# Three of the last four output sets by adding DMAs: x written ahead from SyncE's queue, the gated part added from GpSimd's

## The chip, the cores and the metric

The kernel runs on one core of a Trainium2 chip. The core has TensorE (PE, matrix multiply), VectorE (DVE), ScalarE (ACT), GpSimd (POOL) and SyncE (SP), which here only issues DMAs. DMAs are issued from the instruction queues of SP, ACT and POOL and are carried out by 16 DMA engines that all three share. The metric is the device time of one execution in microseconds; lower is better.

## The reference

With x of 2048 tokens by 576 channels, all in fp32:

```python
xn = _layernorm(x)
s = _A_ref(xn, ...)          # a long convolution along the tokens: y + u * D_skip
g = _silu(_B_ref(xn, ...))   # layernorm, Dense 576 -> 4608, gelu, Dense 4608 -> 576, + b2
return x + s * g
```

So each output element is x plus a gated part, s times silu(z), where z is the output of the multi-layer perceptron (MLP).

## The kernel before, in words

The 2048 tokens are held as 16 sets of 128. The MLP runs over them in two halves (sets 0 to 7, then 8 to 15), each in 12 groups of 384 hidden channels, and each group in two blocks of four sets: 48 slots. A slot has three first-layer units (L595, into PSUM tiles `mxa` and `mxb`) and eight second-layer units (L658); their results are added to `acc` (L668). fp32 operands are split into a high and a low fp32r part, so each product is three matmuls.

The convolution runs beside it in six chunks of 96 channels, through PSUM tiles `cv`, and its matmuls are laid between those of the MLP. Each chunk has steps on TensorE named `x1`, `k1`, `s2` (four times, L1136, each with its own constants `f2t`, loaded at L1024), the inverse (twice, L1178, with constants `g2t`, loaded at L1027) and `i1`. `f2t` has one buffer: a load waits until TensorE is done with the old constants, and TensorE waits for the load. The result of a chunk goes to `s_s` in memory.

The order of all instructions is written out when the program is built: a planner (`Order`) with an estimated time for each step decides what is put next into which engine's queue, and every queue is pinned to that order. Each engine then carries out its own queue in that order and waits there on semaphores. `last_x(k)` counts in the planner as a step of no engine that takes 9 us, for any k.

For the last eight sets, 8 + k with k = 0 to 7, `last_x(k)` loads x into `TM[k]` (L715, on SP's queue), and `last_s(k)` loads s (L720) once the last chunk is done. In the last two slots `finish` ends each set as soon as its `acc` is complete: `act_z` on ScalarE (L738), for sets 8 to 11 a tanh with two products on VectorE (L745, L749), for sets 12 to 15 a silu with one product on VectorE (L743); then `total`, an addition of x on VectorE (L753) and two stores of 64 rows each into the output (L756), both on SP's queue, or for sets 14 and 15 one on SP's and one on ACT's. Set 15 is done in two halves of 288 channels, taken straight from PSUM. Sets 0 to 7 are combined earlier and stored from POOL's queue (L709). The raw weights are loaded on SP's queue (L513, L515, L518), and so is a small copy of `XR` (L569).

Of the kernel before, what the change touches and what calls it, by code (L numbers as in the profile page):

```python
# [9 lines left out]
F32 = mybir.dt.float32  # L10
# [3 lines left out]
OP = mybir.AluOpType  # L14
# [3 lines left out]
L, D, N, F = 2048, 576, 128, 4608  # L18
P = 128
# [12 lines left out]
NXC, NROW = 1, 4  # L32
# [3 lines left out]
TB = 512  # L36
# [3 lines left out]
def dve(n):  # L40
    return 0.075 + 0.00104 * n


def act(n):
    return 0.06 + 0.00098 * n
# [160 lines left out]
def step(eng, dur, fn, need=(), mark=None, cv=0, at=0.0, late=0.0, tbl=None, by=1e9):  # L206
    return dict(eng=eng, dur=dur, fn=fn, need=tuple(need), mark=mark, cv=cv, at=at, late=late, tbl=tbl, by=by)
# [3 lines left out]
def mixer_kernel(ctx, tc, u, log_a_real, a_imag, c_real, c_imag, log_dt, d_skip, w1, b1, w2, b2,  # L211
                 f1, f2, g2, g1, tvals, ident, out, parts=("mlp", "s4d")):
    nc = tc.nc
    sb = ctx.enter_context(tc.tile_pool(name="sb", bufs=1))
# [8 lines left out]
    def dram(ap_of, offset, ap):  # L223
        return bass.AP(tensor=ap_of.tensor, offset=ap_of.offset + offset, ap=ap)
# [135 lines left out]
    def table_memory():  # L360

        t = [sb.tile([P, 2, SB, NV], F32, name="w", bufs=2) for _ in range(2)]
        t = [x.rearrange("p k c t -> p (k c t)") for x in t + [sb.tile([P, 2, SB, 64], F32, name="v")]]
        return [t[k // 3][:, k % 3 * D:(k % 3 + 1) * D] for k in range(8)]
# [326 lines left out]
    def rows_at(t, b, c0, c1):  # L691
        return [dram(t, (b + 16 * y) * D + c0, [[32 * D, 64], [1, c1 - c0]]) for y in range(2)]
# [18 lines left out]
    def last_x(k):  # L711

        if k == 0:
            TM.extend(table_memory())
        nc.sync.dma_start(TM[k], u_s[:, 8 + k, :])  # L715

    def last_s(k):

        m = A2F[:, k * D:(k + 1) * D]
        nc.sync.dma_start(m, s_s[:, 8 + k, :])  # L720
        XS[8 + k] = (TM[k], m)

    TM = []

    def load_identity():
        IDM[0] = sb.tile([P, 32, 24], F32, name="xc", bufs=NXC).rearrange("p b d -> p (b d)")[:, :P]
        nc.sync.dma_start(IDM[0], ident)

    def finish(b, c0, c1, silu, end, z=None):

        c = slice(c0, c1)
        z = acc[:, b - 8, c] if z is None else z
        n = c1 - c0
        T = []

        def act_z():
            T.append(sb.tile([P, D], F32, name="row", bufs=NROW)[:, c])
            nc.scalar.activation(T[0], z, AF.Silu if silu else AF.Tanh, scale=1.0 if silu else 0.5)  # L738

        def mul():  # L740
            s = XS[b][1][:, c]
            if silu:
                nc.vector.scalar_tensor_tensor(s, s, 2.0, T[0], op0=OP.mult, op1=OP.mult)  # L743
            else:
                nc.vector.tensor_mul(s, s, z)  # L745

        def mul2():
            s = XS[b][1][:, c]
            nc.vector.scalar_tensor_tensor(s, T[0], 1.0, s, op0=OP.add, op1=OP.mult)  # L749

        def total():
            x, s = XS[b]
            nc.vector.tensor_add(x[:, c], x[:, c], s[:, c])  # L753
            for y, o in enumerate(rows_at(out, b, c.start, c.stop)):
                queue = nc.scalar if end and y else nc.sync
                queue.dma_start(o, x[64 * y:64 * y + 64, c])  # L756
        st = [step("ACT", act(n), act_z, tbl="silu" if silu else "gelu"), step("DVE", dve(n), mul)]
        if not silu:
            st.append(step("DVE", dve(n), mul2))
        return st + [step("DVE", dve(n), total)]  # L760


    def params():
# [705 lines left out]
    for k in range(8):  # L1469
        tl["steps"].append(step(None, 9.0, lambda k=k: last_x(k), need=[("kg", NB - 1), ("u", NT - 1)], mark=("x8", k)))  # L1470
# [102 lines left out]
    for slot in range(NSLOT):  # L1573
# [3 lines left out]
        n = slot // 2  # L1577
        final = slot >= NSLOT - 2
        for pos in range(NPOS):
            if pos < G:  # L1580
# [9 lines left out]
                if pos == 2:  # L1590
                    BEGUN.clear()
                    k = slot % (2 * NG)
# [14 lines left out]
            else:  # L1607
# [12 lines left out]
                b = 8 + 4 * tb + j  # L1620
                if halves:
                    dh = terms[0][1]
                    od.marks["z", dh] = od.t["PE"] + od.LAT
                    x = od.line()
                    x["steps"] += finish(b, dh * 288, dh * 288 + 288, True, True, cell[0])
                    x["steps"][0]["need"] = (("z", dh), ("s8", b - 8))
                elif last:
                    add = cell[0]
                    chain = [step("DVE", dve(D), lambda: add(0, 2), mark=("acc", slot, j), by=add_by(pos, j))]
                    if final:  # L1630
                        x = el if slot < NSLOT - 1 else od.line()
                        st = finish(b, 0, D, slot == NSLOT - 1, slot == NSLOT - 1 and j > 1)
                        st[0]["need"] = (("acc", slot, j), ("s8", b - 8))
                        x["steps"] += st
                    elif g == NG - 1:
                        for d in range(2):
                            one, two = gate_store(4 * tb + j, d)
                            by = od.t["PE"] + 5.0
                            chain += [step("ACT", act(288), one, tbl="gelu", by=by), step("DVE", dve(288), two, by=by)]
                    od.urgent.append((od.t["PE"], chain))  # L1640
# [61 lines left out]
```

## Time and profile before

| | us |
|---|---|
| median of 3 runs (1101.43 to 1102.87) | 1101.46 |
| the profiled execution, its own time | 1101.22 |
| span of its trace, first to last instruction | 1099.4 |
| TensorE busy in it | 1090.6 |
| VectorE busy | 919.5 |
| ScalarE busy | 696.6 |
| GpSimd busy | 184.2 |

The profiled execution took 1101.22 us, 1.8 us more than its span; it lies 0.24 us under the median. Times in the trace count from the start of the span. TensorE is busy for 99% of it, at a mean granted clock of 0.998 of full speed. Matmuls overlap and their ends are modelled, so the sum of durations is larger than what a stretch takes.

### The profile page before, as it was taken

Reading aid. Unit: us, or ns where it says so; the run is one execution under the profiler, and the core shown is the slowest. Engines: PE = TensorE matmul, PEld = TensorE weight load, DVE = VectorE, ACT = ScalarE, POOL = GpSimd, SP = SyncE. Lnnn points to the kernel's source line nnn. Section 1 sums busy time; section 2 is a strip of 40 time slices with the busy share of each in tenths; the row PEclk is TensorE's granted clock in tenths of the full one; section 3 lists DMA queues with packets and bytes.
Section 4 is the critical chain, followed back from the end, with each engine's and each line's share of the span. In section 5 each row is a group of like instructions: output and inputs, shape, how many; then the busy total and the mean of one; then the engine's idle time right before and its main releaser. Section 6 shows DMA issues by size and latency. Waiting matters only on the chain.

```text
span 1099.4 us, 27205 instructions
## 1 busy us (share of the span) xinstructions
PE 1090.6 (99%) x11447; PEld 954.3 (87%) x11447; DVE 919.5 (84%) x1514; ACT 696.6 (63%) x1040; POOL 184.2 (17%) x254
## 2 busy tenths in 40 slices
PE   9999999999999999999999999999999999999997
PEld 7989899889888888888998888888888888888896
DVE  7798668979998899999999998898998986766356
ACT  6585699866666675676765857566675754324233
POOL 5566211160110100001100000000100012110320
PEclk9999999999999999999999999999999999999999
DMA  8746745734434141355623314241333426453453
GB/s 236 229 150 149 252 141 197 216 73 128 154 119 150 48 112 57 109 120 151 150 56 91 95 56 126 39 146 61 90 92 77 144 65 180 117 177 111 125 148 94
DMA packets 139683, 138.23 MB, mean 126 GB/s; under 512 B 88952, under 2 KB 105016, under 8 KB 138984
## 3 DMA queue, kind: packets, MB, share of 16 engines
q1 hardware_dynamic: 124664, 85.49, 28.9%
q0 software_dynamic: 14336, 50.12, 14.6%
q8 instruction: 89, 1.46, 0.5%
q10 hardware_dynamic: 560, 0.89, 0.3%
q14 instruction: 34, 0.28, 0.1%
HBM read 102.17 MB, written 36.63 MB: 126 GB/s over the span
## 4 chain that ended last, share of the span: by engine, by line
PE 97%; DVE 2%; ACT 1%; issue 0%; DMA 0%; ACTq 0%; DVEq 0%
PE mxb L658 21%; PE mxa L658 21%; PE mxa L595 20%; PE mxb L595 20%; PE cv L1136 3%; PE cv L971 3%; PE cv L1178 2%; PE cv L1204 2%; PE cv L1106 1%; PE cv L1075 1%; PE mxa L610 0%; PE cv L478 0%; DMA acc<-in_A_u_dram 0%; DVE st L403 0%; PE mxa L578 0%
## 5 line engine op out<-in xcount | busy, mean ns | idle before, releaser
L637 DVE TENSOR_TENSOR hl<-h,hh 128x512 fp32r<-128x512 f32 x144 | 98.7, 690 | 90.7 <-ACT hh L634 90.1
L658 PE MATMUL mxb<-w2h,hh 128*128 128x288 f32 x576 | 171.8, 298 | 0.0
L658 PE MATMUL mxa<-w2h,hh 128*128 128x288 f32 x573 | 170.9, 298 | 0.0
L658 PE MATMUL mxb<-w2h,hl 128*128 128x288 f32 x576 | 170.2, 295 | 0.0
L658 PE MATMUL mxb<-w2l,hh 128*128 128x288 f32 x576 | 169.7, 295 | 0.0
L658 PE MATMUL mxa<-w2h,hl 128*128 128x288 f32 x573 | 169.3, 296 | 0.0
L658 PE MATMUL mxa<-w2l,hh 128*128 128x288 f32 x573 | 168.8, 295 | 0.0
L631 ACT ACTIVATE h<-mxa,b1t 128x512 f32<-128x512 f32 x73 | 50.0, 687 | 111.6 <-PE mxa L595 110.8
L658 PEld LDWEIGHTS mxa<-w2h,hh 128*128 128x128 f32 x573 | 107.7, 188 | 6.6 <-issue 3.5
L658 PEld LDWEIGHTS mxb<-w2h,hh 128*128 128x128 f32 x576 | 108.2, 188 | 5.7 <-issue 1.8
L658 PEld LDWEIGHTS mxb<-w2l,hh 128*128 128x128 f32 x576 | 108.2, 188 | 0.6
L658 PEld LDWEIGHTS mxa<-w2l,hh 128*128 128x128 f32 x573 | 107.7, 188 | 0.7
L658 PEld LDWEIGHTS mxb<-w2h,hl 128*128 128x128 f32 x576 | 108.2, 188 | 0.0
L658 PEld LDWEIGHTS mxa<-w2h,hl 128*128 128x128 f32 x573 | 107.6, 188 | 0.0
L872 POOL DMA_DIRECT2D par<-par_s x36 | 27.8, 771 | 463.7 <-DVE mg L915 458.9
L634 ACT ACTIVATE hh<-h 128x512 fp32r<-128x512 f32 x144 | 90.5, 631 | 3.6
L631 ACT ACTIVATE h<-mxb,b1t 128x512 f32<-128x512 f32 x71 | 48.8, 688 | 68.4 <-PE mxb L595 67.7
L668 DVE TENSOR_TENSOR acc<-mxa,acc 128x576 f32<-128x576 f32 x87 | 65.5, 752 | 31.3 <-PE mxa L658 31.1
L595 PE MATMUL mxa<-XH,w1h 128*128 128x512 f32 x284 | 79.1, 400 | 0.0
L595 PE MATMUL mxb<-XH,w1h 128*128 128x512 f32 x280 | 78.0, 400 | 0.8 <-DVE acc L668 0.7
L668 DVE TENSOR_TENSOR acc<-mxb,acc 128x576 f32<-128x576 f32 x88 | 66.1, 751 | 14.7 <-PE mxb L658 14.4
L595 PE MATMUL mxa<-XL,w1h 128*128 128x512 f32 x284 | 76.1, 390 | 0.0
(260 smaller groups left out, 2486.7 us busy)
## 6 DMA issues: line engine op xcount, KB each, us to landing
raw<-in_B_w_dram SPq DMA_DIRECT2D x72, 288.0 KB, 3.4
raw<-in_B_w_dram SPq DMA_DIRECT2D x96, 192.0 KB, 3.5
par_s<-A POOLq DMA_DIRECT2D x4, 2160.0 KB, 8.1
par<-par_s POOLq DMA_DIRECT2D x36, 240.0 KB, 3.4
f2t<-f2q SPq DMA_DIRECT2D x24, 256.0 KB, 3.3
g2t<-g2p SPq DMA_DIRECT2D x24, 256.0 KB, 3.9
bias<-XR SPq DMA_DIRECT2D x42, 128.0 KB, 3.6
raw<-in_B_w_dram SPq DMA_DIRECT2D x48, 96.0 KB, 3.6
```

Of the source, the lines that this page charges most:

```text
L595: nc.tensor.matmul(q, a, b, start=j == 0 and i not in BEGUN, stop=j == len(ops) - 1, skip_group_check=True)
L631: nc.scalar.activation(t, q, AF.Gelu_apprx_tanh, bias=b1t[:, k:k + 1], scale=1.0)
L634: LAST[0] = nc.scalar.activation(hh[:, i], t, AF.Copy)
L637: nc.vector.tensor_sub(hl[:, i], t, hh[:, i].bitcast(F32))
L658: nc.tensor.matmul(q[:, dh, :288], a[:, i, c], b[:, i, d], start=i == 0 and k == 0 and not alone, stop=i == G - 1 and k == 2)
L668: nc.vector.tensor_add(o, q[:, dh:dh + n, :288], b)
L872: nc.gpsimd.dma_start(PAR[b].rearrange("p (g i) k -> p g (i k)", g=4), dram(par_s, (b // 3 * 48 + b % 3 * 4) * NPAR, [[D * NPAR, P], [12 * ...
L971: nc.tensor.matmul(q[32 * g:32 * g + 32, i // 2, i % 2 * 64:i % 2 * 64 + 64], U[:, ri, 4 * g + i, :], v[:, ri, 4 * g + i, :], start=ri == ...
L1075: nc.tensor.matmul(Q[24 * v][:, e], FP[0][r, f, 0], x[r, 12 * e:12 * e + 12], start=n == 0, stop=n == 2, skip_group_check=True)
L1136: nc.tensor.matmul(Q[i][32 * q:32 * q + 32, f, 2 * ri:2 * ri + 2], m[r, 4 * i + q, 32 * ri:32 * ri + 32], A2[r, 4 * p + 2 * i + q // 2, :, ...
L1178: nc.tensor.matmul(QI[q // 2][64 * f:64 * f + 64, q % 2, i], MAT["g2t", p + i // 2][r, i % 2, f, ri], YS[p + i // 2][0][r, i % 2, ri, f], ...
L1204: nc.tensor.matmul(Q[h][64 * y:64 * y + 64, t], g1t.rearrange("p a e -> p (a e)"), A2[:, k:k + 2, 1].rearrange("p i d r -> p i r d"), star ...
```

## The change

For k = 4, 5 and 6 (sets 12, 13 and 14) `last_x` issues, right behind the load of x into `TM[k]`, two stores from `TM[k]` into the rows of the output, on the same queue (SP). At the end `total` no longer adds x on VectorE for these sets and no longer stores from SP or ACT: it issues two DMAs of 64 rows each from GpSimd's queue that add the gated part to the output in memory. In the planner this `total` counts as 1.6 us of GpSimd instead of an addition on VectorE. Beside that, the silu of the two halves of set 15 goes into a buffer of the ring `h32` (2 buffers) instead of the ring `row` (4 buffers).

```diff
@@ last_x
         nc.sync.dma_start(TM[k], u_s[:, 8 + k, :])
+        if k in ADDED:
+            for y, o in enumerate(rows_at(out, 8 + k, 0, D)):
+                nc.sync.dma_start(o, TM[k][64 * y:64 * y + 64])
@@
     TM = []
+    ADDED = 4, 5, 6
@@ finish
         def act_z():
-            T.append(sb.tile([P, D], F32, name="row", bufs=NROW)[:, c])
+            if n < D:
+                T.append(sb.tile([P, TB], F32, name="h32", bufs=2)[:, :n])
+            else:
+                T.append(sb.tile([P, D], F32, name="row", bufs=NROW))
@@
         def total():
             x, s = XS[b]
+            if b - 8 in ADDED:
+                for y, o in enumerate(rows_at(out, b, 0, D)):
+                    nc.gpsimd.dma_start(o, s[64 * y:64 * y + 64], accum_op=OP.add)
+                return
             nc.vector.tensor_add(x[:, c], x[:, c], s[:, c])
@@
-        return st + [step("DVE", dve(n), total)]
+        return st + [step("POOL", 1.6, total) if b - 8 in ADDED else step("DVE", dve(n), total)]
```

## Rows read from the trace of the kernel before

**Rows 1.** The page: the span, and part 1, busy time and share by engine.

```profile
span 1099.4 us, 27205 instructions
PE 1090.6 (99%) x11447; PEld 954.3 (87%) x11447; DVE 919.5 (84%) x1514; ACT 696.6 (63%) x1040; POOL 184.2 (17%) x254
```

**Rows 2.** The chain that ended last, in order of time, its end: start, us, what.

```profile
1093.82 0.17 ACTq L756
...
1094.09 0.42 ACT row L738
...
1095.02 0.46 DVE v L753
```

**Rows 3.** Timeline of SP's queue: start, us, engine, line, what, count.

```profile
956.13 1.44 SPq L715 DMA_DIRECT2D w<-u_s  x1
963.77 0.33 SPq L515 DMA_DIRECT2D raw<-in_B_w_dram  x1
...
966.97 0.58 SPq L715 DMA_DIRECT2D w<-u_s  x1
967.65 0.38 SPq L1024 DMA_DIRECT2D f2t<-f2q  x1
...
975.32 0.75 SPq L715 DMA_DIRECT2D v<-u_s  x1
976.12 0.90 SPq L1027 DMA_DIRECT2D g2t<-g2p  x2
```

**Rows 4.** Timeline of TensorE, two stretches: start, us, engine, line, operation, count.

```profile
973.20 1.60 PE L1136 MATMUL cv<-A,f2t 64*32 64x192 f32 x64
...
989.37 1.83 PE L1178 MATMUL cv<-ys,g2t 32*64 32x96 f32 x128
```

**Rows 5.** DMA issues around 967 us, and all landings of L715 and of L1024.

```profile
w<-u_s SPq DMA_DIRECT2D x1, 288.0 KB, 5.0
...
f2t<-f2q SPq DMA_DIRECT2D x1, 256.0 KB, 4.9
...
DMA to landing us min/median/max: 3.5/4.1/7.4
...
DMA to landing us min/median/max: 2.9/3.3/5.6
```

**Rows 6.** What SP's queue waited for, 950 to 1000 us: total, times, longest.

```profile
SPq L1024 <- DMA f2t<-f2q: 5.2, 2, 4.0
```

**Rows 7.** The output stores of L756: a pair on SP's queue, and the landings of all.

```profile
1092.00 1.11 SPq L756 DMA_DIRECT2D out_dram<-w  x2
...
DMA to landing us min/median/max: 2.3/2.4/2.8
```

**Rows 8.** Timeline of VectorE near the end.

```profile
1090.43 0.75 DVE L743 SCALAR_TENSOR_TENSOR A<-A,row 128x576 f32<-128x576 f32 x1
1091.22 0.76 DVE L753 TENSOR_TENSOR w<-w,A 128x576 f32<-128x576 f32 x1
1091.89 0.75 DVE L743 SCALAR_TENSOR_TENSOR A<-A,row 128x576 f32<-128x576 f32 x1
```

**Rows 9.** GpSimd's queue: output stores of L709, and its transfers from memory to memory.

```profile
L709 POOL DMA_DIRECT2D out_dram<-row x32: 527/533/560, 884.3 to 1077.9; - x32
...
DMA to landing us min/median/max: 1.8/2.1/4.8
...
f2p<-in_f_dram POOLq DMA_DIRECT2D x4, 512.0 KB, 10.8
```

**Rows 10.** Stretches at the end: us, busy by engine, then granted clock, DMA share, GB/s.

```profile
1093.08:1095.08 2.00, 0.00 (x1) 0.00 (x0) 1.70 (x5) 0.41 (x1) 0.00 (x0) 1.00 0.90 199
1095.09:1099.40 4.31, 0.00 (x0) 0.00 (x0) 0.39 (x1) 0.00 (x0) 0.00 (x0) 0.50 0.40 115
```

**Rows 11.** Timeline of TensorE at the start: equal matmuls, earlier and later.

```profile
1.32 6.22 PE L1266 MATMUL mxa<-XL 128*128 128x512 f32 x16 [1.32 <-POOL XL L1259]
...
7.84 2.79 PE L1266 MATMUL mxa<-XL 128*128 128x512 f32 x11
```

## The prediction

> **What bounds the kernel now.** I read the page first: TensorE is busy for 1090.6 of 1099.4 us [rows 1], so whatever keeps TensorE from its next matmul is paid in full, and only what lies behind its last matmul can be saved elsewhere. Its last matmul ends at 1093.08 (TensorE shows no busy time from there on [rows 10]), so 6.3 us of the span lie behind it. The chain of waits then says what fills them: an output store of set 14 is issued from ACT's queue, the silu of the last half set follows it at 1094.09, a product, and the last addition, which ends at 1095.48 [rows 2]; a store that takes 2.4 us to land [rows 7] and the program's end make up the rest. After that I read SP's queue around 956 to 976 us, because the change puts six DMAs there that before stood elsewhere [rows 3], and held it against the times at which TensorE uses what SP loads [rows 4].
>
> **The change, part by part: the end.** Removed from VectorE are three additions (L753) of 0.76 us, those of sets 12, 13 and 14; the second of them stands between two products [rows 8]. The addition of set 12 ended before TensorE did, so what counts is about 1.5 us: set 14's product can start at about 1091.27 instead of 1091.89, and the first half of set 15 is multiplied and summed by about 1092.9. VectorE is then free when TensorE ends at 1093.08. The last silu started at 1094.09, behind set 14's store on ACT's queue [rows 2]; this store goes. The end of VectorE's work can come no sooner than the last matmul plus the silu (0.42), the product (0.47) and the addition (0.46) with their hand-overs, 1093.1 + 1.4 = 1094.5, against 1095.48: at most 1.0 us is won. If the store of set 15's first half stands on ACT's queue ahead of the last silu, its issue (about 0.5 us by the pair in rows 7) costs 0.4 of that. I take 0.7 us.
>
> In place of the removed stores (five on SP, one on ACT) GpSimd issues six adding DMAs. No adding DMA is in the trace. Its issue is bounded by the stores of L709, 0.53 us each, which ran beside VectorE's work and landed in 1.8 to 4.8 us; the far end is a transfer from memory to memory, 10.8 us for 512 KB [rows 9]. An adding DMA has to read its target and write it, so I take a read plus a write of the nearest kind, 2.1 + 2.4 = 4.5 us. Set 14's product ends at 1092.0, its second DMA is issued at about 1092.6 and lands at 1097.1. The plain stores of set 15 are issued at 1094.8 and land at 1097.2. So the adding DMAs are just hidden behind set 15; by the low bound of 1.8 us they gain nothing more, and by the high one of 10.8 us the end comes 6 us later. Their queue is free: GpSimd has nothing after the last L709.
>
> **The change, part by part: the stores issued ahead.** Each store reads the tile that the load just before it fills, so SP waits there until the load has landed; behind it SP's queue stands. That SP waits like this is in the trace: it stood 4.0 us for the landing of one `f2t` before issuing the next [rows 6]. The Trainium skill (page "DMA: Bandwidth & Descriptors", section "Anatomy of one DMA — SWDGE (gpsimd) path") says the same: DMA engines don't wait on semaphores, a wait stands on the sequencer that issues, before dispatch. If the wait could sit in the DMA engines, the queue would move on after 1.2 us and the sum below would hold no stall.
>
> Three places, each a landing plus a pair of stores (1.15 us with its hand-over, [rows 7]):
> - k = 4: the load is issued at 956.13. With the median landing of 4.1 us [rows 5] it is there at 960.2, and SP is through at 961.4. SP's next DMA is issued at 963.77 [rows 3]. Hidden, with 2.4 us to spare.
> - k = 6: the load is issued at 975.32; 4.1 + 1.15 us later, at 980.6, come the two loads of `g2t` that stood at 976.12. Even with the longest landing shown for the other constants, 5.6 us, they are there at 986.7, and TensorE uses them at 989.37 [rows 3 to 5]. Hidden, with 2.7 us to spare.
> - k = 5: the load is issued at 966.97 and landed 5.0 us later, at 971.97. The next in the queue is the load of `f2t` for the first `s2` of the last chunk, issued at 967.65, landed 4.9 us later at 972.55 [rows 3, 5]. TensorE starts on it at 973.20 [rows 4]: 0.65 us of cover. Now it is issued at 971.97 + 1.15 = 973.1, after TensorE already wants it. With a landing between the median (3.3) and that of this very load (4.9) it is there between 976.4 and 978.0; it has 288 KB of stores just ahead in its queue, less than what stood ahead of it before, so I take 3.9, and 977.0. TensorE stands from 973.2 to 977.0: 3.8 us.
>
> The ends of this stall: a landing of x in 3.5 us and of `f2t` in 2.9 gives 970.5 + 1.15 + 2.9 = 974.5, 1.3 us; 5.0 and 5.6 give 978.7, 5.5 us. Nothing later gives it back, since TensorE's queue is full to the end [rows 1]. The copy of `XR` (L569) and all behind it move with the queue; what waits for them on TensorE moves as well. Memory traffic grows by three sets of 288 KB, which is not near any limit.
>
> **The clock.** The granted clock of TensorE was still at full level (2.4 GHz) for 2.0 us after the last matmul and then fell to the half (1.2 GHz) [rows 10]. At the start, after a rest, 16 equal matmuls took 6.22 us, 389 ns each, and the 11 after them 254 ns each [rows 11]. So a rest of 3.8 us probably drops the clock, and a restart from rest cost up to 16 x 0.135 = 2.2 us. For the price of this fall the trace bounds 0 and 2.2 us; the start from rest is the nearer row, but this rest is short, and I take 1.5. The Trainium skill (page "TensorE: Matmul & The Clock Gate", Part 1) states that an idle TensorE falls to the lower clock and regains the higher one by being busy; by that rule alone the price would be something above zero.
>
> **The rivals.**
> - *Stall and clock fall (the forecast).* 3.8 + 1.5 - 0.7 = +4.6 us: span 1104.0, that execution 1105.8, and against the median 1101.46 + 4.6 = 1106.1. For it: the 0.65 us of cover. Chance 0.60.
> - *Stall without a clock fall.* 3.8 - 0.7 = +3.1: 1104.6. Speaks for it: the clock outlived 2.0 us of rest [rows 10]. Chance 0.17.
> - *The other side: no stall worth the name.* The place is the queue behind k = 5. If x lands in 3.5 and `f2t` in 2.9 us, the stall is 1.3 us and, with 0.7 won at the end, 1101.46 + 0.6 = 1102.1; if the order around k = 5 differs so that `f2t` isn't behind the stores, only the end remains: 1101.46 - 0.7 = 1100.8. It decides from an `f2t` that lands before about 976.1 with the clock kept. Against it: x itself landed in 5.0 us there [rows 5], behind weight loads that stay where they are. Chance 0.14, of which 0.03 is faster by over 0.2% (it would take more at the end than the 1.0 us that the chain leaves).
> - *The adding DMAs end last.* At 10.8 us from issue to landing [rows 9] they end 6 us after set 15's stores, beside the stall: about 1112. The Trainium skill (page "DMA: Bandwidth & Descriptors", section "Rules for kernel authors") says that an accumulating DMA reads its destination and writes it later; no run here shows one yet. Against it: only transfers with a far larger size landed that late. Chance 0.09.
>
> **How the numbers follow.** A measurement of this kernel can tell about 0.2%, 2.2 us, from no change. Slower by more (above 1103.7): 0.60 + 0.17 + 0.09 = 0.86; within it 0.11; faster 0.03. The predicted time is that of the likeliest case, 1106.1. The range leaves out the slow adding DMAs and most of the other side: from 1102.4 (x in its median 4.1 us and `f2t` in 2.9 give a stall of 1.9; with the clock kept and the whole 1.0 us won at the end, +0.9) to 1109.2 (stall and clock at their upper ends, 5.5 + 2.2, and nothing won at the end).
>
> **What would show it.** In the profile after: L1024 behind the second store of k = 5 at about 973; an idle time of TensorE of 3 to 5 us before L1136, put down to DMA `f2t`; a slice of half clock just behind it; no such idle time before L1178; the chain at the end through set 15, ending about 0.7 us nearer to the last matmul. I am wrong if L1136 still starts within 1 us of the L595 before it, or if the last landing is one of GpSimd's queue.

## The result, and the profile after

The changed kernel takes 1106.28 us (median of 6 runs, 1104.94 to 1107.84) against 1101.33 before (median of 6): 5.0 us slower, a ratio of 1.0046 (95% interval 1.0035 to 1.0057). The prediction was 1106.1 us and slower, with a range of 1102.4 to 1109.2. The sum was met, but one of its three terms, the end, had the wrong sign.

The profiled execution after took 1107.84 us with a span of 1106.1 (mean granted clock 0.997). What the prediction named first is there. SP's queue after, with the same columns as [rows 3]; L718 are the stores ahead, L1035 is the line of `f2t` now:

```profile
968.09 0.53 SPq L715 DMA_DIRECT2D w<-u_s  x1
971.87 1.13 SPq L718 DMA_DIRECT2D out_dram<-w  x2
973.09 0.54 SPq L1035 DMA_DIRECT2D f2t<-f2q  x1
```

The load of x for k = 5 is issued at 968.09, the stores that wait for it at 971.87, and `f2t` 5.0 us behind the load of x, where it stood 0.68 us behind it before [rows 3]. TensorE's timeline there, as [rows 4], with the idle time ahead of a row in brackets:

```profile
973.93 0.39 PE L595 MATMUL mxb<-XR,w1s 128*128 128x512 f32 x1
977.31 2.82 PE L1147 MATMUL cv<-A,f2t 64*32 64x192 f32 x64 [3.00 <-DMA f2t<-f2q]
```

TensorE stands 3.00 us, and the wait is for `f2t`. The 64 matmuls behind it then take 2.82 us, where they took 1.60 [rows 4], because the clock fell during the rest. The stretches show it (us, busy of TensorE, its weight loads, VectorE, ScalarE and GpSimd, granted clock, DMA share, GB/s):

```profile
974.32:976.67 2.35, 0.00 (x0) 0.00 (x0) 0.94 (x2) 1.32 (x2) 0.00 (x0) 1.00 0.62 167
976.67:980.08 3.41, 2.77 (x65) 1.77 (x65) 1.40 (x4) 0.49 (x1) 2.30 (x5) 0.50 0.29 63
980.08:984.00 3.92, 3.92 (x35) 3.92 (x30) 1.50 (x4) 0.49 (x1) 0.40 (x1) 1.00 0.89 259
```

At full level (2.4 GHz) for the first 2.35 us of the rest, then at the half (1.2 GHz) until 980.08, of which TensorE worked 2.77 us.

The end of the changed kernel, from VectorE, ScalarE, GpSimd and TensorE in turn (L750 is the product, L764 the addition, L762 the adding DMAs, L767 the plain stores):

```profile
1099.33 0.46 DVE L750 SCALAR_TENSOR_TENSOR A<-A,h 128x288 f32<-128x288 f32 x1 [1.11 <-ACT h L745]
1099.83 0.46 DVE L764 TENSOR_TENSOR v<-v,A 128x288 f32<-128x288 f32 x1
...
1098.25 0.53 ACTq L767 DMA_DIRECT2D out_dram<-v  x1
1098.89 0.41 ACT L745 ACTIVATE h<-cv 128x288 f32<-128x288 f32 x1 [1.72 <-PE cv L658]
...
1094.44 5.14 POOL L762 DMA_DIRECT2D out_dram<-A  x6 [10.68 <-DVE A L750]
...
1098.12 0.29 PE L658 MATMUL cv<-w2h,hl 128*128 128x288 f32 x1
```

The last matmul ends at 1098.41, VectorE at 1100.29: 1.88 us behind it, where it was 1095.48 - 1093.08 = 2.40 before [rows 2, 10]. So VectorE did win 0.5 us. But the span ends at 1106.1, 7.7 us behind the last matmul, where it was 6.3: the end is 1.4 us longer, not shorter. The landings say why. The issues between 1098 and 1102 us, and below them those of set 15 before, of 1093 to 1097 us (KB each, median us to landing; on SP's queue only the landing of the first half was recorded, in both kernels):

```profile
out_dram<-A POOLq DMA_DIRECT2D x2, 144.0 KB, 5.4
out_dram<-v SPq DMA_DIRECT2D x2, 72.0 KB, 4.8
out_dram<-v ACTq DMA_DIRECT2D x2, 72.0 KB, 4.3
```

```profile
out_dram<-v SPq DMA_DIRECT2D x2, 72.0 KB, 2.3
out_dram<-v ACTq DMA_DIRECT2D x2, 72.0 KB, 2.4
```

The same plain stores of set 15 took up to twice as long to land while the adding DMAs were under way: 3.8 to 4.9 us where it was 2.3 to 2.5. The very last on ACT's queue, issued at 1100.32, took 3.8. In all, the two profiles differ by 6.7 us: 1.05 us had passed before the change acts (the last L595 ahead of the stall starts at 973.93, before at 972.88; in a second profile of the changed kernel, below, at 972.35, so this is a spread between executions), 3.06 at the stall (977.31 against 973.20, less the 1.05), 1.22 by the lower clock (the last matmul is 5.33 us later, L1147 only 4.11), and 1.4 at the end.

The mean granted clock and the span together sort the six runs. Three of them have a mean clock of 0.997 and spans of 1104.9, 1105.2 and 1106.1; three have 0.999 and spans of 1102.9, 1103.7 and 1104.0. The kernel before has 0.998, with a low clock only behind its last matmul [rows 10]. So the clock probably fell in the middle in three of these six runs, where the span was 1.9 us longer (1105.4 against 1103.5, means of three). Only the profiled execution shows the fall itself, and a mean of 0.997 alone does not prove one: in add_late_x, below, which has no stall, three of eleven runs have 0.997 at spans no longer than the others'.

### The profile page after: what moved, and what is told of

Its sections match the earlier page's. It is cut to its first block, busy times and chain, and to the rows that moved or that the text cites. A ratio compares the mean times of both kernels' runs of the same rounds, so it can differ in the third digit from the quotient of the medians.

```text
span 1106.1 us, 27214 instructions
## 1 busy us (share of the span) xinstructions
PE 1092.1 (99%) x11447; PEld 955.2 (86%) x11447; DVE 919.5 (83%) x1511; ACT 697.0 (63%) x1040; POOL 188.6 (17%) x260
## 4 chain that ended last, share of the span: by engine, by line
PE 95%; DMA 2%; DVE 2%; SPq 1%; issue 0%; ACT 0%; ACTq 0%; DVEq 0%
PE mxb L658 21%; PE mxa L658 20%; PE mxa L595 20%; PE mxb L595 20%; PE cv L1147 3%; PE cv L982 3%; PE cv L1189 2%; PE cv L1215 2%; PE cv L1086 1%; PE cv L1117 1%; DMA acc<-in_A_u_dram 0%; DMA h<-in_B_b_dram 0%; DMA f2t<-f2q 0%; DMA w<-u_s 0%; PE mxa L578 0%
## 5 line engine op out<-in xcount | busy, mean ns | idle before, releaser
L595 PE MATMUL mxa<-XH,w1h 128*128 128x512 f32 x284 | 79.2, 400 | 0.0
L595 PE MATMUL mxb<-XH,w1h 128*128 128x512 f32 x280 | 77.9, 400 | 0.7 <-DVE acc L668 0.7
L595 PE MATMUL mxa<-XL,w1h 128*128 128x512 f32 x284 | 76.1, 390 | 0.0
```

The lines of the kernel that those rows point to most:

```text
L595: nc.tensor.matmul(q, a, b, start=j == 0 and i not in BEGUN, stop=j == len(ops) - 1, skip_group_check=True)
```

## The experiments

Two theories stood against each other. The first, that of the prediction: SP's queue holds `f2t` behind the wait of k = 5, TensorE stands, and the clock may fall. The second: the adding DMAs at the end are the loss, and the stores ahead are harmless. All times are compared with runs of the kernel before on the same chip: 1101.12 us for ahead_k5, ahead_k46, add_late_x and plain_pool, 1101.24 for ahead_prev, add_late_45, changed_again and pool_sum. These are the names of the runs, in brackets at each of the paragraphs below.

**Only the stores ahead of k = 5 (ahead_k5).** In the kernel before:

```diff
         nc.sync.dma_start(TM[k], u_s[:, 8 + k, :])
+        if k in (5,):
+            for y, o in enumerate(rows_at(out, 8 + k, 0, D)):
+                nc.sync.dma_start(o, TM[k][64 * y:64 * y + 64])
```

> The kernel before, with the two stores of x issued ahead for k = 5 alone; the end is left as it was, so the same rows are written again there with the sum. My theory (SP's queue stands behind k = 5 and holds f2t, TensorE stands for it): TensorE idle 2.5 to 3.5 us before the first s2 of the last chunk, +3.0 us, and 1.0 to 2.0 us more in those executions whose granted clock falls: 1104.3 to 1106.3 beside about 1101.3 before. Rival (the loss of the change is at its end, in the adding DMAs): no difference, within 0.5 us of before.

Measured: 1106.15 us (1105.02 to 1106.71), ratio 1.0043 (1.0031 to 1.0056). One pair of stores costs as much as the whole change. The queue, the landing of `f2t`, VectorE's L706 and TensorE (L1139 is the first `s2` here):

```profile
966.73 0.58 SPq L715 DMA_DIRECT2D w<-u_s  x1
970.55 1.17 SPq L718 DMA_DIRECT2D out_dram<-w  x2
971.82 0.54 SPq L1027 DMA_DIRECT2D f2t<-f2q  x1
...
DMA to landing us min/median/max: 4.3/4.3/4.3
...
975.66 0.56 DVE L706 TENSOR_TENSOR row<-row 128x384 f32<-128x384 f32 x1
...
976.29 2.82 PE L1139 MATMUL cv<-A,f2t 64*32 64x192 f32 x64 [3.24 <-DVE row L706]
```

TensorE stands 3.24 us. The row puts the wait down to VectorE's L706, which ended just before, at 976.22. But the first `s2` does not need L706: in the kernel before it starts at 973.20 [rows 4], and L706 comes after it:

```profile
975.88 0.56 DVE L706 TENSOR_TENSOR row<-row 128x384 f32<-128x384 f32 x1
```

What came last is `f2t`: issued at 971.82, it landed 4.3 us later, at about 976.15. TensorE starts 0.1 us behind that, as it does in the changed kernel, where `f2t` was issued at 973.09, took 4.1 us, and the row names it. The clock fell as well, and stayed down longer than in the changed kernel:

```profile
975.38:982.20 6.82, 5.91 (x77) 4.92 (x78) 2.45 (x6) 0.98 (x2) 2.70 (x5) 0.50 0.61 146
```

Of this stretch TensorE worked 5.91 us at half the clock; the last matmul is 5.73 us later than before and the first `s2` 3.09, so the fall cost 2.6 us here. Why it stayed down longer than in the changed kernel stays open. The first theory holds; its stall is in the upper part of what was expected, and the fall cost more than the 1 to 2 us expected. The end of this kernel is as before: 6.1 us behind the last matmul (1098.81 to 1104.9).

**Only the stores ahead of k = 4 and k = 6 (ahead_k46).** The same edit with `if k in (4, 6)`.

> The kernel before, with the two stores of x issued ahead for k = 4 and k = 6, not for k = 5; the end is left as it was. My theory (both stalls of SP's queue are covered, 2.4 and 2.7 us to spare): within 0.5 us of before, and no idle time of TensorE before the first s2 or the inverse of the last chunk. Rival (each pair of stores ahead costs alike, by its 288 KB or by holding the queue): two thirds of what three would cost, +2 to +3.5 us.

Measured: 1100.65 us (1100.07 to 1102.03), ratio 0.9997 (0.9988 to 1.0006): no difference. SP's queue at k = 6 is held just as it is at k = 5:

```profile
974.89 0.37 SPq L715 DMA_DIRECT2D v<-u_s  x1
978.48 1.14 SPq L718 DMA_DIRECT2D out_dram<-v  x2
979.67 1.11 SPq L1030 DMA_DIRECT2D g2t<-g2p  x2
...
988.95 0.38 PE L1181 MATMUL cv<-ys,g2t 32*64 32x96 f32 x10
```

The two loads of `g2t` go out at 979.67 instead of about a microsecond behind the load of x, and TensorE still starts on them at 988.95 straight behind the L595 before it. A hold of 3.6 us, as of 3.8 at k = 5, and no price that could be measured: it is the slack of what stands next in the queue that decides.

**The landing or the stores? (ahead_prev)** At the same place in the queue, the stores of x of k = 4 instead of k = 5, so that nothing has to be waited for:

```diff
         nc.sync.dma_start(TM[k], u_s[:, 8 + k, :])
+        if k == 5:
+            for y, o in enumerate(rows_at(out, 8 + 4, 0, D)):
+                nc.sync.dma_start(o, TM[4][64 * y:64 * y + 64])
```

> The kernel before, with one pair of stores issued ahead at the same place in SP's queue as in ahead_k5 (behind the load of k = 5), but of x of k = 4, which landed some 6 us earlier, so that nothing is waited for. The end is as before. My theory (the wait for the landing of x, about 3.8 us, holds the queue; the issue of two stores is 1.15 us): f2t is issued at about 968.8 instead of 971.8, TensorE stands 0.5 to 1.2 us, the clock stays: +0.5 to +1.2 us over before. Rival (the 288 KB of stores just ahead of f2t delay it, waiting or not): most of the 3 us stall stays, +2.5 us or more.

Measured: 1101.40 us (1100.57 to 1102.28), ratio 0.9999 (0.9990 to 1.0008).

```profile
967.55 0.58 SPq L715 DMA_DIRECT2D w<-u_s  x1
968.17 1.17 SPq L718 DMA_DIRECT2D out_dram<-w  x2
969.44 0.53 SPq L1027 DMA_DIRECT2D f2t<-f2q  x1
...
973.98 1.60 PE L1139 MATMUL cv<-A,f2t 64*32 64x192 f32 x64 [0.15 <-DMA f2t<-f2q]
```

With 288 KB of stores just ahead of it, `f2t` is there 0.15 us too late, and the clock stays. The expectation of at least 0.5 us was too high. Of the 3.24 us of ahead_k5, 3.1 go with the wait for the landing of x, and next to nothing with the stores themselves.

**The changed kernel without the hold (add_late_x).** The six stores of x moved to where x landed long ago:

```diff
     def last_s(k):
         m = A2F[:, k * D:(k + 1) * D]
         nc.sync.dma_start(m, s_s[:, 8 + k, :])
+        if k in ADDED:
+            for y, o in enumerate(rows_at(out, 8 + k, 0, D)):
+                nc.sync.dma_start(o, TM[k][64 * y:64 * y + 64])
```

(and taken out of `last_x`).

> The changed kernel, with the six stores of x moved from behind the load of x to behind the load of s in last_s, where x landed long ago and nothing has to be waited for; the adding DMAs stay. My theory: no stall and no clock fall in the middle, only what the end of the changed kernel showed, 7.7 us behind the last matmul instead of 6.3: +1.4 us, about 1102.7. Rival (the adding DMAs are the main loss): 1105 or more. Other rival (they gain what was planned, and the 1.4 us were chance): 1100.6.

Measured: 1102.41 us (1102.11 to 1103.47), ratio 1.0012 (1.0003 to 1.0020). No idle time before the first `s2`, no fall of the clock, and 8.0 us behind the last matmul (1093.33 to 1101.3). So without the hold 1.3 us are still lost, at the end, with an interval of 0.3 to 2.2, where 0.7 should have been won. The next kernel tells whether it is the adding.

**The same six DMAs without adding (plain_pool).** In the last kernel, `accum_op=OP.add` left out, so the output lacks x in sets 12 to 14:

> As add_late_x, but the six DMAs of GpSimd's queue at the end store the gated part plainly instead of adding it, so in sets 12 to 14 the output lacks x. If reading and writing the target is what makes the end long: their landing falls from 4.9 to about 2.5 us and the end behind the last matmul from 7.7 to about 5.8 us, 1.9 us under add_late_x, about 1100.8. If GpSimd's queue itself is (its issues took 0.9 to 1.8 us in the changed kernel): issues and landings as in add_late_x and the same time within 0.3 us.

Measured: 1100.66 us (1100.15 to 1102.13), ratio 0.9995 (0.9987 to 1.0004), 1.75 us under the last. GpSimd's DMAs in both, first with the addition, then plain: durations (min, median, max in ns) and landings (likewise in us), the sixth issue by itself, and what the packets of GpSimd's queue came to between 1085 and 1100 us (packets, MB, share of the 16 DMA engines):

```profile
L762 POOL DMA_DIRECT2D out_dram<-A x6: 890/1286/1784, 1089.4 to 1093.1; - x6
DMA to landing us min/median/max: 3.3/4.9/5.9
...
1093.11 1.39 POOL L762 DMA_DIRECT2D out_dram<-A  x1
...
q0 software_dynamic: 480, 0.89, 42.3%
```

```profile
L762 POOL DMA_DIRECT2D out_dram<-A x6: 529/529/529, 1088.7 to 1092.4; - x6
DMA to landing us min/median/max: 2.3/2.8/2.9
...
1092.43 0.53 POOL L762 DMA_DIRECT2D out_dram<-A  x1
...
q0 software_dynamic: 288, 0.89, 23.4%
```

And the plain stores of set 15 beside them, again first with the addition:

```profile
out_dram<-v SPq DMA_DIRECT2D x2, 72.0 KB, 4.1
out_dram<-v ACTq DMA_DIRECT2D x2, 72.0 KB, 4.1
```

```profile
out_dram<-v SPq DMA_DIRECT2D x2, 72.0 KB, 3.1
out_dram<-v ACTq DMA_DIRECT2D x2, 72.0 KB, 2.7
```

It is the addition, not GpSimd's queue. An adding DMA of 144 KB takes 4.9 us to land instead of 2.8, and the stores beside it land later too. The record of its issue is longer as well, 1.29 us instead of 0.53, but no issue comes later for it: these records overlap, the DMAs of a set start 0.54 to 0.57 us apart (plain 0.53), and the sixth starts 0.22 us ahead of the end of the last matmul with the addition (1093.11 of 1093.33) and 0.23 without (1092.43 of 1092.66). What grew is the work of the DMA engines: for the same 0.89 MB the queue's packets took 42.3% of the 16 engines in 15 us instead of 23.4%. The plain version also estimates what the change could have won had the adding been free: 0.5 us, with an interval that takes in zero.

**Two sets added, the last one not (add_late_45).** As the kernel without the hold, with `ADDED = 4, 5`:

> As add_late_x, but only sets 12 and 13 are added by DMAs; set 14 is summed on VectorE and stored from SP's and ACT's queues as before. If set 14's adding DMAs, the last two, are what collides with the stores of set 15: their landing comes back to about 2.4 us and the end behind the last matmul from 8.0 to about 6.0 us, about 1100.5. If any adding DMA near the end does it: 7 us or more behind the last matmul, 1101.5 or more.

Measured: 1101.19 us (1100.37 to 1103.01), ratio 1.0001 (0.9992 to 1.0010), 5.9 us behind the last matmul (1094.15 to 1100.1). The plain stores of set 15:

```profile
out_dram<-v SPq DMA_DIRECT2D x2, 72.0 KB, 3.4
out_dram<-v ACTq DMA_DIRECT2D x2, 72.0 KB, 3.2
```

The loss of 1.3 us is gone, so it goes with set 14's pair, the adding DMAs that are still under way beside the last stores. The landings did not come all the way back, 3.4 and 3.2 us instead of 2.3 and 2.4, but no loss shows. Nor does a gain: with set 14's addition back on VectorE the kernel is level with the one before, within an interval of 1 us either way.

**The changed kernel once more (changed_again).**

> The changed kernel again, beside the others on one chip. If stall (3.0 us), clock fall (1 to 3 us where it comes) and end (+1.3 us as in add_late_x) simply add: 1105.4 to 1108, above ahead_k5 by about 1.3 us. If part of the end is hidden when the stall is there: no more than ahead_k5, about 1106.1.

Measured: 1107.08 us (1106.03 to 1108.81), ratio 1.0054 (1.0042 to 1.0067), 0.9 us above ahead_k5. By the times this does not decide: the two ran on different chips, the intervals of their ratios overlap, and the first series of the changed kernel (1106.28) lies 0.1 us above ahead_k5. The profiles do. The end is 7.8 us behind the last matmul (1097.52 to 1105.3), against 6.1 in ahead_k5 and 8.0 in add_late_x, so the stall hides next to nothing of the end and the terms add. In its profile TensorE stands 3.31 us; `f2t` landed at 975.9, so this wait too is for `f2t`:

```profile
972.35 0.39 PE L595 MATMUL mxb<-XR,w1s 128*128 128x512 f32 x1
976.04 2.76 PE L1147 MATMUL cv<-A,f2t 64*32 64x192 f32 x64 [3.31 <-DVE row L706]
```

**GpSimd adds x itself (pool_sum).** No stores ahead and no adding DMAs. The main lines, against the changed kernel; the stores ahead are taken out of `last_x`, and the planner counts this `total` as 3.2 us of GpSimd:

```diff
-    ADDED = 4, 5, 6
+    ADDED = 4, 5
@@ total
+                nc.gpsimd.tensor_add(x, x, s)
                 for y, o in enumerate(rows_at(out, b, 0, D)):
-                    nc.gpsimd.dma_start(o, s[64 * y:64 * y + 64], accum_op=OP.add)
+                    nc.gpsimd.dma_start(o, x[64 * y:64 * y + 64])
...
-                queue = nc.scalar if end and y else nc.sync
+                queue = nc.scalar if end and y and c0 else nc.sync
```

> No stores ahead and no adding DMAs: x of sets 12 and 13 is added by GpSimd's own addition and stored from its queue, set 14 by VectorE; of the stores of sets 14 and 15 only the very last stays on ACT's queue, so that no store stands ahead of the last silu. My theory (the adding on VectorE costs little, and the DMAs that read their target are what lengthens the end): the end behind the last matmul 5.3 to 5.8 us instead of 6.3, 0.5 to 1.0 us under before, about 1100.4, which can't be told from before with certainty. Rival (GpSimd's addition slows VectorE or comes last): 6.5 us or more behind the last matmul, 1101.5.

Measured: 1102.27 us (1101.40 to 1103.60), ratio 1.0009 (1.0000 to 1.0018), 7.2 us behind the last matmul. My expectation failed, and the rival was right. VectorE, GpSimd and ScalarE:

```profile
1092.51 2.32 DVE L762 TENSOR_TENSOR v<-v,A 128x576 f32<-128x576 f32 x1
...
1092.79 1.42 POOL L758 TENSOR_TENSOR w<-w,A 128x576 f32<-128x576 f32 x1
...
1093.63 0.41 ACT L742 ACTIVATE h<-cv 128x288 f32<-128x288 f32 x1 [1.34 <-PE cv L658]
```

VectorE's addition of set 14 took 2.32 us instead of 0.76, beside GpSimd's of set 13, and the products and additions of set 15 came after it: VectorE ended at 1096.56, 3.0 us behind the last matmul (1093.52) instead of 2.4. The other half of the edit did what it was meant to: with no store ahead of it on ACT's queue the last silu starts 0.1 us behind the last matmul. The Trainium skill (page "SBUF — State Buffer", section "Who interferes with whom") says that a VectorE instruction with two inputs in SBUF contends with a GpSimd instruction that reads SBUF; this trace agrees, 2.32 against 0.76 us.

## Why the prediction was right, point by point

**The three places in SP's queue: right.** k = 4 and k = 6 were said to be hidden and k = 5 not; ahead_k46 and ahead_k5 show exactly that (0.9997 and 1.0043).

**The size of the stall: 3.8 us said, 3.0 to 3.3 measured.** The step that was too large is the landing of x. I took 5.0 us from [rows 5]; it was through 3.8 us after its issue in the changed kernel (968.09 to 971.87). Its 5.0 before had the loads of `f2t` and of `XR` issued right behind it, and now the queue stands behind it; over the traces kept, this load of x took 3.7 to 3.9 us where the queue stood (3 traces) and 4.5 to 5.1 where `f2t` followed at once (6). The other two parts fit: the pair of stores took 1.2 us, and `f2t`, for which I took 3.9, needed 4.1 (issued at 973.09, landed at about 977.2).

**The clock: 1.5 us said, 1.2 to 2.6 measured where it fell.** In the two profiles of the changed kernel the fall cost 1.2 and 1.6 us (in the second the last matmul is 4.44 us later than before, the first `s2` 2.84); in ahead_k5, where it stayed down twice as long, 2.6. The 1.5 was chosen between bounds, and the upper one, 2.2 us from the start of the program [rows 11], was read wrongly: the view gives the granted clock as full there,

```profile
2.00:4.00 2.00, 2.00 (x6) 1.56 (x5) 0.00 (x0) 0.73 (x1) 0.04 (x1) 1.00 0.98 243
```

(columns as above), so those slower matmuls do not show what a low clock costs. That 1.5 came out near is in part luck. The rival without a clock fall was put at 1104.6; the three of the first six runs that probably had none took 1104.94 to 1105.76. So forecast and rival both seem to have happened, from run to run. By the same reading the clock fell in four of the five runs of changed_again (mean clocks 0.996 and 0.997 against one of 0.998), in seven of eleven with the first six; chances of 0.60 and 0.17 can't be faulted by that.

**The end: 0.7 us won said, 1.3 us lost measured. This is the step that failed.** Its first half held: VectorE's end came 0.5 us nearer to the last matmul, and the store on ACT's queue ahead of the last silu cost its 0.5 us, as feared (the silu starts at 1098.89, the last matmul ends at 1098.41). The landing of an adding DMA was also near: 4.5 us taken, 4.9 measured as the median, 5.6 for the last. Their issue was near too: they start 0.54 to 0.57 us apart, plain ones 0.53. The term that failed is the landing of set 15's plain stores, behind which the adding DMAs were to be hidden: I took 2.4 us, as if the adding DMAs left them alone, and they took 3.8 to 4.9. The last one on ACT's queue landed 1.5 us later after its issue than before, which is more than the 0.5 won on VectorE. plain_pool and add_late_45 show that the loss goes away with the addition, or with set 14's part of it, and in plain_pool GpSimd's queue took 23.4% of the DMA engines instead of 42.3%. That the stores wait for these engines is the likely reason; how the engines share their time among queues was not looked at.

**The total was met by luck, because errors nearly cancel:** the stall was 0.7 us too large and the clock, as a mean over the first six runs, 0.6, while the end was 2.0 us too good. The sum of the terms as measured, 3.1 + 0.9 (1.9 in half of the runs) + 1.3 = 5.3, stands against 5.0 and, in the second series, 5.8 us.

**The rival that the adding DMAs end last** fell as it was put: they landed in at most 5.9 us, not 10.8, and the last landing recorded is that of a store of set 15, issued at 1100.32 and landed 3.8 us later, at 1104.1. It was close: the last adding DMA, issued at 1098.19, landed 5.6 us later, at 1103.8.

## What to carry to other kernels

A store of what has just been loaded, put into the same queue as the load, held that queue here until the load had landed; before placing one, look up what stands next in the queue and how long before its use it lands. A hold of 3.6 us cost nothing that could be measured where the next load had microseconds to spare, and one of 3.8 cost 3 us, plus a fall of the clock, where it had 0.65. At the same place, a store whose data had landed some 6 us before cost nothing that could be measured. Work that is taken off VectorE at the end and given to adding DMAs can slow the very stores that end the kernel: count those stores' landing again.

## What the runs showed of the hardware that was not expected

- An adding DMA of 144 KB (64 rows of 2304 bytes) landed in 3.3 to 5.9 us, a plain one of the same shape in 2.3 to 2.9; six of them made 480 packets against 288. Its issue is recorded with 0.89 to 1.78 us against 0.53, yet the next one starts 0.54 to 0.57 us after it. Plain stores of 72 KB beside them landed in 3.8 to 4.9 us; in the kernel before it was 2.3 to 2.5.
- A rest of TensorE of 3.0 to 3.3 us led to a fall of the granted clock in all three traces kept of it; the mean clocks and spans of the other runs make it likely that it did not in every one. After a fall it was at half level from 976.67 to 980.08 in one profile, and from 975.38 to 982.20 in another.
- VectorE's addition of two 128x576 fp32 tiles took 2.32 us instead of 0.76 while GpSimd added two of its own. The delay can also fall on the other side: GpSimd's addition of set 12, started at 1089.34 beside a product of VectorE that kept its 0.76 us, took 2.06 us against 1.42 for set 13.
